# A ConvNeXt-V2 block on one core: the DRAM copy of the normalised image laid out by row pair and channel

## The chip, the core and the metric

The kernel runs on one core of a Trainium2 chip. The core has a matrix engine (TensorE, "PE" in the profile, with its weight loads as "PEld"), a vector engine (VectorE, "DVE"), an activation engine (ScalarE, "ACT"), a general engine (GpSimd, "POOL") and a queue processor (SyncE, "SP") that here only issues DMAs. Sixteen DMA engines move data between DRAM and the on-chip memory (SBUF); PE's results land in PSUM. The metric is device time in microseconds (us): the median of three runs was 1463.72 us before the change (1463.25 to 1465.25).

## The reference, cut to what matters

The input `x` has 512 x 512 pixels of 96 channels in bf16.

```python
out = sum(xp[:, i:i+H, j:j+W, :] * dw[i, j] for i in range(3) for j in range(3))  # depthwise 3x3
h = _layernorm(out, axis=-1)                    # over the 96 channels of a pixel
h = jnp.einsum('bhwc,ce->bhwe', h, w1)          # 96 -> 384
h = _gelu(h)
gx = jnp.sqrt((h * h).sum(axis=(1, 2), keepdims=True) + 1e-6)   # per channel, over ALL pixels
nx = gx / (gx.mean(axis=-1, keepdims=True) + 1e-6)
h = grn_gamma * (h * nx) + grn_beta + h
h = jnp.einsum('bhwe,ec->bhwc', h, w2)          # 384 -> 96
return x + h
```

The sum in `gx` runs over the whole image, so nothing can be put out before every pixel has gone through the first matmul and the gelu. That splits the kernel into two passes.

## The kernel before

**Blocks and quads.** The image is cut into 64 blocks of 8 rows (index `d`). Each block is two quads of 4 rows (index `b` or `q`, 128 in all).

**The first pass** works on a block in steps. Four DMAs load its pixels (`load_x`, tile `xin`). DVE transposes them 32 by 32 (`turn_x`, tile `xT`). PE does the 3x3 convolution on 32 x 32 tiles (`conv_taps`), and the result is stored as `y_bf` in two halves `ee`, each [128, 3, 512]: partition p = 32 q + 2 c + k holds row k of the row pair q, and channel c of sixteen; the three planes are the groups G of 32 channels, and `ee` is the channel's parity. POOL squares it (`stage_sq`), PE sums over channels (`stage_stats`), DVE forms the variance, POOL takes the inverse root by Newton steps (`stage_rstd`, `stage_newton`), DVE transposes the result (`stage_turn`, tile `rt`). SP writes it to DRAM in four small DMAs (`stage_rows`) and reads it back spread over the partitions in four more (`stage_bcast`, tile `rbc`). Statistics, rows and broadcasts are done for batches of two blocks. POOL then multiplies (`stage_norm`, tile `yn`, one instruction per half).

**The copy.** `yn` has channels and rows mixed on the partitions, while the matmul with `w1` needs 96 channels on 96 partitions. So SP writes `yn` to DRAM (`stage_write`: one DMA for the half `ee` = 0, two for `ee` = 1, whose row pairs are rotated by two) and reads it back as `ynT`, [96, 4, 512] for each quad (`stage_read`, `read_yn`: two DMAs per quad, one for each row pair). In DRAM the copy lies as `[d][plane ee*3+G][pair][32 x 512]`: six planes, 128 KB apart. The ring `yn_ring` holds six quads.

**The MLP.** PE multiplies a quad by `w1` and ACT applies the gelu (`mlp_units`, six units per quad, tile `g`). DVE (`bn_stats`) or PE (`gram_next`) gather the sums of squares. Every third quad ("whole") is also stored to DRAM as it is, in three DMAs of 512 KB (`store_next`, tensor `g_dram`), one per slot.

**The second pass** goes through the 128 quads in an order written out beforehand (`ORDER`). Whole quads are loaded from `g_dram` (POOL's queue, 1.5 MB); five are still held; for the other 85, less three that are kept on chip, `ynT` is read again (SP's queue, `read_yn`) and matmul and gelu are done again (`recompute`). PE multiplies by the scaled `w2` (`stage_mm2`), DVE adds the input and the bias (`xb`), and SP stores the result (`stage_out`).

**What sets the order.** Every instruction of the first pass stays in program order on its engine. A planner (`put`, L802 to L838) fills slots; a slot holds one MLP quad. For block `d` with its norm in slot s, an odd one: the write is in s+1, the reload of the even quad in s+2, of the odd quad in s+3, their MLPs in s+4 and s+5. Rows of a batch are two slots after its last statistics, broadcasts three, the first norm four. Inside a slot the loop from L857 on fixes what SP issues, one after the other. From slot 13 on, an odd slot has: x loads, a store, the reload of the even quad, rows; an even slot: the reload of the odd quad, broadcasts, first write, a store, two more writes. Before slot 13 ("early") the reloads come first and the x loads after the writes.

The built program gives SP's DMAs eight completion counters in turn: a DMA is issued only when the eighth one before it has landed, whatever else it waits for.

Of the kernel before, what the change touches and what calls it, by code (L numbers as in the profile page):

```python
# [12 lines left out]
GR = 4  # L13
# [40 lines left out]
def kernel(  # L54
# [13 lines left out]
    bf16 = x.dtype  # L68
    assert bf16 == mybir.dt.bfloat16

    B, H, W, C = x.shape
# [11 lines left out]
    QW = GR * 128  # L83
    NQ = GR * W // QW
    dram = ctx.enter_context(tc.tile_pool(name="dram", bufs=1, space=bass.MemoryType.DRAM))
    yn_dram = dram.tile([ND, 2 * NI, 4, 32 * W], bf16, name="yn_dram")
    r_dram = dram.tile([len(BATCHES), R8 * BATCH * W], bf16, name="r_dram")

    TAIL0 = NBLK - NTAIL
# [25 lines left out]
    def quad_out(flat_ap):  # L115
        return flat_ap.rearrange("p (g r m) -> p g r m", r=GR, m=MB)

    PLANE = 4 * 32 * W

    def read_yn(eng, t, q):  # L120
        base = yn_dram[q // 2]
        for h in range(2):
            eng.dma_start(out=t[:C, 2 * h:2 * h + 2, :].rearrange("c r w -> c (r w)"),
                          in_=bass.AP(base.tensor, base.offset + (2 * (q % 2) + h) * 32 * W,
                                      [[2 * W, 16], [PLANE, 2 * NI], [1, 2 * W]]))

    consts = ctx.enter_context(tc.tile_pool(name="consts", bufs=1))
    prepool = ctx.enter_context(tc.tile_pool(name="pre", bufs=1))
# [49 lines left out]
    with ExitStack() as p1:  # L178
# [242 lines left out]
            pool.dma_start(out=bet_bf[:], in_=grn_beta.rearrange("(j p) -> p j", p=128))  # L421

        def setup_ynt():
            for t in yn_ring:
                pool.memset(t[C:128, :, :].rearrange("p r w -> p (r w)").bitcast(f32), 0.0)

        def setup_mlp():
# [219 lines left out]

        def stage_write(d, ee):
            yn = yns.pop((d, ee))
            base = yn_dram[d]  # L650
            step = 64 if ee else 128
            for p0 in range(0, 128, step):
                sp.dma_start(out=bass.AP(base.tensor, base.offset + ee * NI * PLANE + (p0 + 64 * ee) % 128 * W,
                                         [[W, step], [PLANE, NI], [1, W]]),
                             in_=yn[p0:p0 + step, :, :])

        def stage_read(b):
            t = yn_ring[b % NYT]
            read_yn(sp, t, b)
            ynts[b] = t  # L660

        bsts = {}
        ents = {}
# [140 lines left out]
        def put(s, what, v):  # L804
            at.setdefault((s, what), []).append(v)
# [5 lines left out]
        for k, (d0, n) in enumerate(BATCHES):  # L811
            for d in range(d0, d0 + n):
                quick = 2 * d + 1 not in mlp_slots
                put(2 * d + 1 if quick else 2 * d + 2, "sqa" if quick else "sqp", d)
                put(2 * d + 2, "staty", d)
                last_s = 2 * d + 2 if quick else 2 * d + 3
                put(last_s, "statq", d)
            ramp = 2 * (d0 + n) <= RAMP
            if ramp:
                put(last_s, "chain", k)  # L820
                put(last_s + 1, "spread", k)
            else:
# [29 lines left out]
        def next_x(s):  # L852
            if s % 2 and (s + 7) // 2 <= ND:
                load_x((s + 7) // 2)

        alone = 0
        for s in range(last_slot + 1):  # L857
            get = lambda kind: at.get((s, kind), [])
            early = s < FIRST_MLP + 6
            if not early:  # L860
                next_x(s)
            if early or s % 2 == 0:
                for b in get("read"):
                    stage_read(b)
            for k in get("bcast"):
                stage_bcast(k)
            for d in get("write"):
                stage_write(d, 0)
            store_next()
            for d in get("write"):  # L870
                stage_write(d, 1)
            if early:
                next_x(s)
            elif s % 2:
                for b in get("read"):
                    stage_read(b)
            for k in get("rows"):
                stage_rows(k)
            for k in get("newton"):
                stage_rstd(k, pool)  # L880
                stage_newton(k, pool)
# [47 lines left out]
            else:  # L929
# [160 lines left out]
```

## Time and profile before

| What | Value |
|---|---|
| Median of three runs | 1463.72 us |
| The profiled execution | 1462.48 us, of which its span 1460.6 us |
| Busy: PE, ACT, POOL, DVE | 1334.5, 1333.3, 1299.0, 1080.6 us |
| First pass with all stages at work | about 100 to 850 us |
| Second pass | about 950 to 1460 us |
| SP's hardware queue (q1) | 178044 packets, 318.50 MB, 69.6% of 16 engines |
| `ynT<-yn_dram` | 420 DMAs of 192 KB |
| `yn_dram<-yn` | 64 DMAs of 384 KB, 128 of 192 KB |
| `g_dram<-g` | 114 DMAs of 512 KB |

Times on the profile are microseconds from the start of the span. A row of a group names line, engine, operation, output and input tiles. "L36" is the helper that records every instruction of the first pass, so groups are told apart by their tiles. "SPq" is SP's queue: an instruction there is the issue of a DMA, not the transfer. A line of the list of waits reads: who waited, for whom, total us, number of times, longest us. The share of DMA is the mean busy share of the 16 engines.

### The profile page before, as it was taken

To read this page: it belongs to the slowest core of one execution; us is meant where nothing else is said; L and a number is where in the kernel's file an instruction comes from. 1 tells how busy PE (TensorE), PEld (TensorE's weight loads), DVE (VectorE), ACT (ScalarE), POOL (GpSimd) and SP (SyncE) were. 2 spreads that over 40 slices of the span, in tenths; PEclk is the share of its full clock that TensorE was granted. 3 is DMA by queue.
4 is the path that set the end of the run, shared out by engine and by line. 5 is a ranking of instruction groups with operands and counts; after the bars stand their busy time and mean duration, and the time that the engine had idled before them with its cause. 6 is when DMAs were issued, how large, how long until landed. Compare 5 with 4: busy or idle time off the path is not lost.

```text
span 1460.6 us, 55999 instructions
## 1 busy us (share of the span) xinstructions
PE 1334.5 (91%) x24212; PEld 871.7 (60%) x24212; DVE 1080.6 (74%) x2052; ACT 1333.3 (91%) x1235; POOL 1299.0 (89%) x899
## 2 busy tenths in 40 slices
PE   7879999999999999989999987889999989899998
PEld 3445555555555555555555554567777667666676
DVE  5768988988889898888889878745555545455455
ACT  4879999999999999999999999989999888888897
POOL 3499999999999999999999995489999999899997
PEclk8899999999999999999999999999999999999999
DMA  7779899998899998999899766499999999999997
GB/s 175 212 219 283 275 286 274 277 287 269 271 299 272 277 290 268 281 280 275 261 275 299 228 190 192 162 355 331 344 373 391 393 383 362 378 378 370 395 366 303
DMA packets 194103, 430.82 MB, mean 295 GB/s; under 512 B 39184, under 2 KB 88944, under 8 KB 188992
## 3 DMA queue, kind: packets, MB, share of 16 engines
q1 hardware_dynamic: 178044, 318.50, 69.6%
q0 software_dynamic: 15616, 108.29, 19.9%
q8 instruction: 190, 3.11, 0.9%
q10 hardware_dynamic: 196, 0.45, 0.1%
q14 instruction: 57, 0.47, 0.1%
HBM read 265.70 MB, written 161.45 MB: 292 GB/s over the span
## 4 chain that ended last, share of the span: by engine, by line
PE 42%; DMA 22%; ACT 18%; POOL 7%; DVE 4%; issue 3%; SPq 2%; ACTq 0%; DVEq 0%; POOLq 0%
PE PS L36 42%; ACT g L36 13%; DMA out_dram<-o_sb 11%; DMA ynT<-yn_dram 7%; ACT y_bf L36 4%; POOL xb L339 3%; DMA xin<-in_x_dram 3%; SPq L36 2%; POOL yn L36 2%; DVE bst L36 2%; DVE o_sb L36 1%; POOL ysq L36 1%; DMA rbc<-r_dram 1%; ACT xT L36 1%; ACT ysq L36 0%
## 5 line engine op out<-in xcount | busy, mean ns | idle before, releaser
L36 ACT ACTIVATE g<-PS 128x1024 bf16<-128x1024 f32 (+1 forms) x722 | 705.5, 1055 | 34.3 <-PE PS L36 20.2
L36 DVE BATCH_NORM_STATS2 bst<-g 128x6 f32<-128x512 bf16 x885 | 547.0, 677 | 46.8 <-ACT g L36 46.7
L36 PE MATMUL PS<-ynT,w1p 128*128 128x512 bf16 x1920 | 544.8, 381 | 39.0 <-ACT g L36 23.0
L36 ACT ACTIVATE gr<-PS 128x1536 bf16<-128x1536 f32 x348 | 485.8, 1450 | 47.6 <-PE PS L36 42.3
L36 DVE TENSOR_TENSOR o_sb<-PS,xb 128x384 bf16<-128x384 f32 x512 | 275.7, 557 | 244.8 <-PE PS L36 172.2
L36 POOL TENSOR_TENSOR yn<-y_bf,rbc 128x1536 bf16<-128x1536 bf16 x124 | 382.3, 3104 | 14.2 <-DMA rbc<-r_dram 13.2
L339 POOL TENSOR_TENSOR xb<-xr,B2c 128x1536 f32<-128x1536 bf16 x118 | 368.4, 3132 | 17.2 <-DVE o_sb L36 15.7
L36 POOL TENSOR_TENSOR ysq<-y_bf 128x1536 bf16<-128x1536 bf16 x120 | 327.1, 2747 | 38.1 <-DVE y_bf L36 38.1
L36 PEld LDWEIGHTS <-gr 128*128 128x128 bf16 x4152 | 206.6, 99 | 82.6 <-issue 31.5
L36 PE MATMUL PS<-xT,Wq 32*32 32x511 bf16 (+1 forms) x9216 | 235.9, 396 | 10.7 <-DVE xT L36 3.8
L36 PEld LDWEIGHTS <-w1p 128*128 128x128 bf16 x1920 | 148.4, 98 | 152.6 <-issue 89.2
L36 PE MATMUL PS<-W2s,gr 128*128 128x96 bf16 x4080 | 216.6, 207 | 23.6 <-DVE o_sb L36 23.3
L36 PE MATMUL PS<-w1p,ynT 128*128 128x384 bf16 (+2 forms) x1272 | 192.7, 273 | 27.6 <-ACT g L36 22.2
L36 PEld LDWEIGHTS <-Wq 32*32 32x32 bf16 x9216 | 100.2, 89 | 142.8 <-issue 64.8
L36 PEld LDWEIGHTS <-g 128*128 128x128 bf16 x2626 | 161.9, 98 | 34.2 <-issue 4.2
L36 PE MATMUL PS<-g 128*128 128x128 bf16 (+1 forms) x2386 | 173.2, 222 | 1.8 <-DVE warm L36 1.2
L36 PEld LDWEIGHTS <-ynT 128*128 128x128 bf16 x1272 | 102.0, 97 | 105.2 <-issue 82.6
L36 ACT ACTIVATE y_bf<-PS 128x1024 bf16<-128x1024 f32 (+1 forms) x141 | 137.4, 984 | 25.2 <-PE PS L36 25.2
L36 DVE STREAM_TRANSPOSE xT<-xin 128x576 f32<-128x576 f32 (+1 forms) x195 | 145.0, 771 | 6.2 <-DMA xin<-in_x_dram 4.9
L36 PEld LDWEIGHTS <-gl 128*128 128x128 bf16 x1824 | 89.4, 98 | 32.3 <-issue 9.4
L36 PE MATMUL PS<-W2s,gl 128*128 128x96 bf16 x1824 | 96.5, 206 | 7.7 <-DVE o_sb L36 7.5
L36 DVE CAST y_bf<-PS 128x512 bf16<-128x512 f32 x115 | 78.1, 679 | 5.8 <-PE PS L36 5.1
(108 smaller groups left out, 571.6 us busy)
## 6 DMA issues: line engine op xcount, KB each, us to landing
ynT<-yn_dram SPq DMA_DIRECT2D x420, 192.0 KB
g_dram<-g SPq DMA_DIRECT2D x114, 512.0 KB
gl<-g_dram POOLq DMA_DIRECT2D x38, 1536.0 KB, 11.3
xin<-in_x_dram SPq DMA_DIRECT2D x253, 216.0 KB
out_dram<-o_sb SPq DMA_DIRECT2D x127, 384.0 KB
xr<-in_x_dram POOLq DMA_DIRECT2D x123, 384.0 KB, 7.1
yn_dram<-yn SPq DMA_DIRECT2D x64, 384.0 KB
yn_dram<-yn SPq DMA_DIRECT2D x128, 192.0 KB
```

The lines of the kernel that those rows point to most:

```text
L36: r = f(*a, **k)
L339: pq.tensor_tensor(out=xb[:], in0=grp[q]["xr"][:], in1=bias[:, None, :].to_broadcast([128, PXP, C]), op=ALU.add)
```

## The change

- The copy in DRAM is now `[quad][row pair][channel][2 rows x 512]`, with the channels in the order in which `ynT` has them. A row pair is 192 KB in one piece.
- A block is written with six DMAs: two for `ee` = 0 (one for each row of the pairs, 64 partitions two apart), four for `ee` = 1 (32 partitions each).
- A block is reloaded with one DMA of 768 KB into a pair of ring places; the ring is allocated as three pairs. In the second pass a quad is one DMA of 384 KB.
- Both quads are reloaded in slot s+2. From slot 13 on an odd slot issues: rows, the reload, x loads, broadcasts, a store; an even slot: six writes, a store. Broadcasts move from the third slot after the statistics to the second, behind the rows of the same slot.
- A whole quad is stored in two DMAs of 768 KB, one per slot, at the end of what SP issues in the slot.

```diff
-    yn_dram = dram.tile([ND, 2 * NI, 4, 32 * W], bf16, name="yn_dram")
+    yn_dram = dram.tile([NBLK, 2, C, 2 * W], bf16, name="yn_dram")
...
-    def read_yn(eng, t, q):
-        base = yn_dram[q // 2]
-        for h in range(2):
-            eng.dma_start(out=t[:C, 2 * h:2 * h + 2, :].rearrange("c r w -> c (r w)"),
-                          in_=bass.AP(base.tensor, base.offset + (2 * (q % 2) + h) * 32 * W,
-                                      [[2 * W, 16], [PLANE, 2 * NI], [1, 2 * W]]))
+    def read_yn(eng, t, q, n=1):
+        base = yn_dram[q]
+        eng.dma_start(out=t[:C].rearrange("c r w -> c (r w)"),
+                      in_=bass.AP(base.tensor, base.offset, [[2 * W, C], [2 * W * C, 2 * n], [1, 2 * W]]))
...
-    yn_ring = [prepool.tile([128, GR, W], bf16, name=f"ynT{i}") for i in range(NYT)]
+    yn_pairs = [prepool.tile([128, R8, W], bf16, name=f"ynT{i}") for i in range(NYT // 2)]
+    yn_ring = [yn_pairs[i // 2][:, GR * (i % 2):GR * (i % 2) + GR, :] for i in range(NYT)]
...
         def stage_write(d, ee):
             yn = yns.pop((d, ee))
-            base = yn_dram[d]
-            step = 64 if ee else 128
-            for p0 in range(0, 128, step):
-                sp.dma_start(out=bass.AP(base.tensor, base.offset + ee * NI * PLANE + (p0 + 64 * ee) % 128 * W,
-                                         [[W, step], [PLANE, NI], [1, W]]),
-                             in_=yn[p0:p0 + step, :, :])
+            base = yn_dram[2 * d]
+            np_ = 64 if ee else 128
+            for k in range(2):
+                for p0 in range(0, 128, np_):
+                    pair = (p0 // 32 + 2 * ee) % 4
+                    sp.dma_start(out=bass.AP(base.tensor, base.offset + pair * C * 2 * W + ee * NI * 2 * W + k * W,
+                                             [[2 * NI * 2 * W, np_ // 2], [2 * W, NI], [1, W]]),
+                                 in_=yn[p0 + k:p0 + np_:2, :, :])
-        def stage_read(b):
-            t = yn_ring[b % NYT]
-            read_yn(sp, t, b)
-            ynts[b] = t
+        def stage_read(d):
+            read_yn(sp, yn_pairs[d % (NYT // 2)], 2 * d, 2)
+            for b in (2 * d, 2 * d + 1):
+                ynts[b] = yn_ring[b % NYT]
...
-                put(last_s + 3, "bcast", k)
+                put(last_s + 2, "bcast", k)
...
+                put(s + 2, "read", d)
                 for b in (2 * d, 2 * d + 1):
-                    put(s + 2 if ramp else s + 2 + b % 2, "read", b)
...
-            if not early:
+            if early:
+                reads()
+            else:
+                rows()
+                reads()
                 next_x(s)
-            if early or s % 2 == 0:
-                for b in get("read"):
-                    stage_read(b)
+            for d in get("write"):
+                for ee in range(2):
+                    stage_write(d, ee)
+            if early:
+                store_next()
+                next_x(s)
+                rows()
             for k in get("bcast"):
                 stage_bcast(k)
-            for d in get("write"):
-                stage_write(d, 0)
-            store_next()
-            for d in get("write"):
-                stage_write(d, 1)
-            if early:
-                next_x(s)
-            elif s % 2:
-                for b in get("read"):
-                    stage_read(b)
-            for k in get("rows"):
-                stage_rows(k)
+            if not early:
+                store_next()
...
-                n = NCH * QW * NQ // 3
+                n = NCH * QW * NQ // 2
...
-                    stores.extend((b, h) for h in range(3))
+                    stores.extend((b, h) for h in range(2))
```

More of the change, by code (lines that the diff above doesn't have):

```diff
@@ L116, in quad_out @@
         return flat_ap.rearrange("p (g r m) -> p g r m", r=GR, m=MB)
-    PLANE = 4 * 32 * W
-    def read_yn(eng, t, q):
-        base = yn_dram[q // 2]
-        for h in range(2):
-            eng.dma_start(out=t[:C, 2 * h:2 * h + 2, :].rearrange("c r w -> c (r w)"),
-                          in_=bass.AP(base.tensor, base.offset + (2 * (q % 2) + h) * 32 * W,
-                                      [[2 * W, 16], [PLANE, 2 * NI], [1, 2 * W]]))
+    def read_yn(eng, t, q, n=1):
+        base = yn_dram[q]
+        eng.dma_start(out=t[:C].rearrange("c r w -> c (r w)"),
+                      in_=bass.AP(base.tensor, base.offset, [[2 * W, C], [2 * W * C, 2 * n], [1, 2 * W]]))
     consts = ctx.enter_context(tc.tile_pool(name="consts", bufs=1))
@@ L423, in setup_ynt @@
         def setup_ynt():
-            for t in yn_ring:
+            for t in yn_pairs:
                 pool.memset(t[C:128, :, :].rearrange("p r w -> p (r w)").bitcast(f32), 0.0)
@@ L859, with reads, rows @@
             early = s < FIRST_MLP + 6
-            if not early:
-                next_x(s)
-            if early or s % 2 == 0:
-                for b in get("read"):
-                    stage_read(b)
+            def reads():
+                for d in get("read"):
+                    stage_read(d)
+            def rows():
+                for k in get("rows"):
+                    stage_rows(k)
+            if early:
[3 more added lines that the diff above has]
+                reads()
+                next_x(s)
+            for d in get("write"):
[5 more added lines that the diff above has]
+                rows()
             for k in get("bcast"):
                 stage_bcast(k)
-            for d in get("write"):
-                stage_write(d, 0)
-            store_next()
-            for d in get("write"):
-                stage_write(d, 1)
-            if early:
-                next_x(s)
-            elif s % 2:
-                for b in get("read"):
-                    stage_read(b)
-            for k in get("rows"):
-                stage_rows(k)
+            if not early:
+                store_next()
             for k in get("newton"):
```

## The prediction

> **What bounds the kernel now.** I read the stages first, the first pass (200 to 800 us) and the second (1000 to 1440 us). Columns after the span: busy time of PE, weight loads, DVE, ACT and POOL, granted clock, DMA share, GB/s.
>
> ```profile
> 200.00:800.00 600.00, 560.70 (x11667) 341.18 (x11644) 537.69 (x989) 573.70 (x614) 570.90 (x417) 1.00 0.91 278
> 1000.00:1440.00 440.00, 414.63 (x6056) 307.45 (x6055) 232.58 (x433) 401.65 (x289) 411.71 (x249) 0.99 1.02 375
> ```
>
> The first pass has no slack engine: ACT 96%, POOL 95%, PE 93%, DMA 91%. In the second the DMA engines never rest (1.02), so only their work counts there. Next, who waits between 300 and 870 us:
>
> ```profile
> PE PS L36 <- DMA ynT<-yn_dram: 10.6, 13, 2.1
> POOL yn L36 <- DMA rbc<-r_dram: 9.2, 10, 1.6
> PEld L36 <- DMA ynT<-yn_dram: 3.7, 4, 0.9
> ```
>
> PE stands 14.3 us before a reload of yn. The whole run's list has the same two totals, so none of it lies before 300 us. What it costs shows in the norms on POOL, two per block of 8 rows, in two windows:
>
> ```profile
> L36 POOL TENSOR_TENSOR yn<-y_bf,rbc x25: 3079/3106/3124, 126.1 to 288.2; 128x1536 bf16<-128x1536 bf16 x25
> L36 POOL TENSOR_TENSOR yn<-y_bf,rbc x77: 3089/3105/3128, 303.7 to 828.6; 128x1536 bf16<-128x1536 bf16 x77
> ```
>
> The first row is 12 blocks in 162.1 us, 13.51 each; the second 38 blocks in 524.9 us, 13.81 each. The first pace is POOL's own work (a block's squares and norms, and half of a Newton chain). The loss against it is 0.30 x 38 = 11.5 us. Last, SP's timeline, POOL's norm and the PE wait about 405 us (start, duration; a row merges several issues and the gaps between):
>
> ```profile
> 398.69 3.54 SPq L36 DMA_DIRECT2D xin<-in_x_dram  x4
> 402.33 0.37 SPq L36 DMA_DIRECT2D g_dram<-g  x1
> 403.33 2.79 SPq L36 DMA_DIRECT2D ynT<-yn_dram  x4
> 406.22 1.48 SPq L36 DMA_DIRECT2D yn_dram<-yn  x1
> 407.80 0.43 SPq L36 DMA_DIRECT2D g_dram<-g  x1
> 408.32 1.95 SPq L36 DMA_DIRECT2D yn_dram<-yn  x2
> ```
> ```profile
> 398.21 6.18 POOL L36 TENSOR_TENSOR yn<-y_bf,rbc 128x1536 bf16<-128x1536 bf16 x2
> ```
> ```profile
> 409.69 1.02 PE L36 MATMUL PS<-ynT,w1p 128*128 128x512 bf16 x4 [0.41 <-DMA ynT<-yn_dram]
> ```
>
> POOL ends the block's norms at 404.39. SP, in order, is still issuing four reloads of the block before; the last write is out at 410.27, 5.9 us after the norm. The loop norm, write, reload, MLP has run out of slack because SP is late.
>
> **The change, part by part.** Issue costs on SP (min/median/max ns, 200 to 800 us):
>
> ```profile
> L36 SPq DMA_DIRECT2D ynT<-yn_dram x174: 541/589/1893, 210.8 to 800.0; - x174
> L36 SPq DMA_DIRECT2D yn_dram<-yn x132: 400/610/2307, 203.6 to 793.8; - x132
> L36 SPq DMA_DIRECT2D xin<-in_x_dram x176: 412/519/2134, 206.7 to 797.4; - x176
> L36 SPq DMA_DIRECT2D g_dram<-g x88: 339/428/1696, 204.3 to 798.0; - x88
> ```
>
> *SP's issues, per block.* Writes go from 3 to 6: +3 x 0.61 = +1.8 us (bounds 1.2 at the row's minimum, 6.9 at its maximum; the median, as the new ones are halves and quarters of those). Reloads go from 4 to 1: -3 x 0.59 = -1.8. The one reload has four times the pieces of an old one; an issue of it is bounded by 0.54 and 1.89, and I take 0.59, since the 384 KB write with as many pieces lies in a row whose median is 0.61. Stores go from 2 to 1.33: -0.3. Sum -0.3 us, nil on its own.
>
> *Order.* In the odd slot the reload is now first (behind the rows, every second block) and waits there for the writes to land. Behind it on SP stand four x loads, four broadcasts in every second block, and a store. The x loads are used four slots, 27 us, after their issue, and nobody waits for xin between 300 and 870 us: free. The broadcasts are issued right behind the x loads, a slot earlier than now, and are due two slots later; if that cover went, the 9.2 us above would stay. The rows are no longer behind x loads and reloads. The writes now have only broadcasts and a store before them, so I let them go out when their norm is ready: two at the end of the first half, four within 4 x 0.61 = 2.4 us of the second, against 5.9 above. That is 3.5 us of slack back per block. Today's lists show 28.9 us of SP waiting for writes to land, in 44 blocks; with the reload standing first I expect 100 to 150. That is waiting on an engine with nothing due.
>
> *What this wait does to the DMA engines.* Their work is 0.91 x 600 / 44 = 12.4 us per block. Between the landing of the writes and the first piece of the reload they have only what SP put behind the writes, a store half of 768 KB (2.8 us at 278 GB/s), in two slots of three. Uncovered, the hole is bounded by 0 and by 3.3 us, the one broadcast in the chain of waits that ran alone (issue to landing 3.27 us at 860 us, little data). I take 3 us in a third of the blocks, 1.0 on average: 12.4 + 1.0 = 13.4, just under POOL's 13.51. So POOL sets the pace again, and the loss of 11.5 us goes.
>
> *Ring in pairs.* The read of a block needs the pair of three blocks before; its MLP ended two slots earlier. The waits in the built program name the same matmul as before for each half in the second pass: no false dependency. Cost 0; bound 0 to 1.4 us once, at the ramp, where the first quad now waits for 384 KB more (at 278 GB/s).
>
> *Stores in halves.* Nobody waits for g_dram in the lists; 0.
>
> *Second pass.* One reload of 384 KB instead of two of 192. Here SP's eight completion counters, used in turn, make a DMA wait for the eighth before it: 22.6 + 9.2 + 9.1 + 8.9 = 49.8 us of waiting for out and ynT landings, which mostly goes. It gains nothing while the DMA engines are full; full they were. What could count is the pieces themselves, still 2 KB, now side by side instead of 128 KB apart. Queues in this stage:
>
> ```profile
> q0 software_dynamic: 13376, 94.31, 56.9%
> q1 hardware_dynamic: 31090, 69.84, 44.3%
> ```
>
> q0 moves 1.66 MB per percent. Of q1, 108 stores of 384 KB are 42.5 MB, at q0's rate 25.6%; the reloads' 26.7 MB took the other 18.7%, or 1.43 MB per percent. Bounds: at q0's rate they would take 16.1%, a gain of 2.6% of 440 us = 11.4 us (13 over the whole pass of 510 us); as much in the other direction. I take 0, as size, partitions and pieces per engine are those of before.
> [...] No run here shows a pitch's effect yet.
>
> *Sum.* -11.5 in the first pass from 300 to 829 us, -0.5 for the blocks behind it, 0 elsewhere: -12.0. The profiled execution is 1462.48 us (span 1460.6 and 1.9 around it), so 1450.5 there; the median of the runs is 1.2 above it, so **1452 us**.
>
> **The rivals.**
> *The hole decides (slower).* Place: SP, at the reload's wait in each odd slot. If a block's writes land late because the pieces are small, and no store covers, the engines idle 1.9 us per block rather than 1.0: 14.3 us per block, 0.5 above today's 13.81, x 54 blocks = +26, less the 3.5 us of slack won once: about 1486. It decides from a hole of 13.81 - 12.4 = 1.4 us. For it: DMA at 0.91, so little room. Against: two slots in three have a store behind the writes.
> [...] The trace agrees that these issues cost 0.6 us each, but it also has three reload issues that go; that size gets 0.02, inside the hole's 0.18.
> *The layout pays (faster).* Contiguous pieces bring the reload to q0's rate: 1452 - 13 = 1439. For it: the 14% lower rate. Against: 96 partitions, unchanged, may be the cause.
> *Nothing moves.* The slack is eaten by something else in the loop (newton, rows), or reloads get slower in the second pass by what the first wins: 1464. For it: ACT and POOL leave 4 to 5% in all. Against: 125 to 300 us ran at 13.51 with the same loop.
>
> **How the numbers follow.** My forecast 0.60, layout 0.10, hole 0.18, nothing 0.12 (0.07 within 0.2%, 0.05 above). 0.2% is 2.9 us, about what a measurement here tells from no change. The forecast's own range is 1446 to 1459, with 0.02 of its 0.60 within 0.2%. So faster 0.58 + 0.10 = 0.68, same 0.09, slower 0.23. The range leaves out the stronger half of the hole, a hole of over about 1.9 us (0.10), and the best of the layout (0.06): 1438 to 1484.
>
> **What would show it.** Right: norms 13.5 us per block through 829 us, PE's waits for ynT between 300 and 870 us from 14.3 to under 3, those of POOL for rbc near 0, writes issued within 3 us of the norm, SP's waits for yn_dram up to 100 or more, second pass at 375 GB/s within 1%. Wrong: GB/s under 278 and a falling DMA share between 200 and 800 us with blocks over 13.8 (the hole), or a second pass shorter or longer than 510 us by more than 4.

## The result and the profile after

The changed kernel took 1567.66 us (median of four runs, 1566.34 to 1575.45) against 1463.49 us for the kernel before on the same chip: a ratio of 1.0735, 95% interval 1.0681 to 1.0789. The prediction was 1452 us, with 1438 to 1484 as its range. It was wrong in sign and by 116 us.

The sum `gx`, which ends the first pass, stands at 1030.7 us instead of 934.4. From there to the end it is 536.4 us instead of 526.2. So 96 us were lost in the first pass and 10 in the second (profiled executions: 1568.82 us with a span of 1567.0, against 1462.48 and 1460.6).

The stages first, as in the prediction; the second row is moved by 96 us with the pass. Columns after the span: busy PE, weight loads, DVE, ACT, POOL, granted clock, DMA share, GB/s. The changed kernel:

```profile
200.00:800.00 600.00, 524.91 (x10345) 306.29 (x10344) 482.13 (x880) 513.15 (x545) 508.85 (x376) 0.95 0.92 248
1100.00:1536.00 436.00, 402.43 (x5845) 297.63 (x5843) 224.86 (x418) 388.23 (x279) 399.86 (x242) 0.99 1.02 368
```

Every engine does less in the same time, and the DMA engines are as busy as before (0.92 against 0.91) while they move 248 GB/s instead of 278. That pair, a full share at a lower rate, will matter below. The granted clock is 0.95 where it was 1.00. Who waits, 300 to 870 us (total us, times, longest), and the norms on POOL:

```profile
PEld L36 <- DMA ynT<-yn_dram: 39.2, 19, 3.7
PE PS L36 <- DMA ynT<-yn_dram: 37.5, 19, 3.6
POOL yn L36 <- DMA rbc<-r_dram: 32.5, 10, 4.0
POOL yn L36 <- DMA yn_dram<-yn: 30.8, 7, 6.2
```
```profile
L36 POOL TENSOR_TENSOR yn<-y_bf,rbc x72: 3089/3105/3132, 304.3 to 848.0; 128x1536 bf16<-128x1536 bf16 x72
```

PE's 37.5 us and its weight loads' 39.2 are the same 19 moments, so PE stands about 39 us before a reload where the kernel before has 11. (The prediction's 14.3 added 10.6 and 3.7 in the same way.) POOL waits 63 us, half of it for a buffer of `yn` whose write has not landed. The norms: 72 are 36 blocks, and from the first norm of the first to the second norm of the last (3.1 us behind its first) there are 543.7 us, so 540.6 / 35 = 15.4 us per block, where 13.51 was forecast.

SP's waits between 200 and 800 us, first two lines of the kernel before, then the changed kernel and its timeline near the place that the prediction shows:

```profile
SPq L36 <- DMA yn_dram<-yn: 28.9, 34, 1.9
...
SPq L36 <- DMA xin<-in_x_dram: 4.5, 14, 0.7
```
```profile
SPq L36 <- DMA ynT<-yn_dram: 73.6, 39, 3.7
SPq L36 <- DMA xin<-in_x_dram: 59.4, 125, 1.8
SPq L36 <- DMA yn_dram<-yn: 41.6, 54, 3.4
```
```profile
408.83 5.66 SPq L36 DMA_DIRECT2D yn_dram<-yn  x6
...
416.21 0.32 SPq L36 DMA_DIRECT2D ynT<-yn_dram  x1
...
419.46 7.48 SPq L36 DMA_DIRECT2D yn_dram<-yn  x6
```

POOL's norms there, and PE's wait (in brackets the idle time before the row and what ended it):

```profile
396.89 6.17 POOL L36 TENSOR_TENSOR yn<-y_bf,rbc 128x1536 bf16<-128x1536 bf16 x2
412.97 6.18 POOL L36 TENSOR_TENSOR yn<-y_bf,rbc 128x1536 bf16<-128x1536 bf16 x2 [4.50 <-DMA yn_dram<-yn]
```
```profile
407.88 1.89 PE L36 MATMUL PS<-ynT,w1p 128*128 128x512 bf16 x4 [3.26 <-DMA ynT<-yn_dram]
```

The norm that ended at 403.06 is written from 408.83 to 414.49: its last write leaves SP 11.4 us later, where it was 5.9 before and 2.4 was forecast. That is a bad block: the median over the blocks from 200 to 800 us is 8.4 us, against 5.7 before. And SP waits 133 us in all for reloads and x loads, of whose data it has no need: all 164 of these waits end on the completion counter that the DMA to be issued uses itself. SP's DMAs use eight such counters in turn: of the 1241 behind the first eight, 1237 have that of the eighth before (1357 of 1361 in the kernel before). In 1239 of the 1241 every landing record of the DMA before on the same counter lies ahead of the end of the issue, and in the other two all but one, which the trace does not have. The chain of waits shows how the two meet (start, duration, what):

```profile
402.26 9.30 DMA xin<-in_x_dram
...
412.85 3.27 DMA yn_dram<-yn
...
416.21 6.29 DMA ynT<-yn_dram
...
422.54 3.01 PE PS L36 x61
```

An x load that takes 9.3 us lets a write go, the write lets the reload go, and PE waits for the reload. The x loads that nobody was to wait for stand in the chain.

### The profile page after: what moved, and what is told of

Its sections match the earlier page's. It is cut to its first block, busy times and chain, and to the rows that moved or that the text cites. A ratio compares the mean times of both kernels' runs of the same rounds, so it can differ in the third digit from the quotient of the medians.

```text
span 1567.0 us, 55627 instructions
## 1 busy us (share of the span) xinstructions
PE 1371.0 (87%) x24212; PEld 877.3 (56%) x24212; DVE 1085.1 (69%) x2052; ACT 1338.4 (85%) x1235; POOL 1298.9 (83%) x896
## 4 chain that ended last, share of the span: by engine, by line
PE 39%; DMA 36%; ACT 13%; DVE 4%; issue 3%; POOL 3%; SPq 2%; ACTq 0%; DVEq 0%; POOLq 0%
PE PS L36 39%; DMA out_dram<-o_sb 14%; DMA ynT<-yn_dram 9%; ACT g L36 8%; DMA xin<-in_x_dram 7%; DMA yn_dram<-yn 3%; ACT y_bf L36 2%; SPq L36 2%; DVE bst L36 1%; DMA g_dram<-g 1%; DVE o_sb L36 1%; POOL yn L36 1%; ACT xT L36 1%; POOL ysq L36 1%; DMA rbc<-r_dram 1%
## 5 line engine op out<-in xcount | busy, mean ns | idle before, releaser
L36 PE MATMUL PS<-ynT,w1p 128*128 128x512 bf16 x1920 | 558.8, 391 | 87.5 <-DMA ynT<-yn_dram 62.6
L336 POOL TENSOR_TENSOR xb<-xr,B2c 128x1536 f32<-128x1536 bf16 x118 | 368.4, 3131 | 24.4 <-DVE o_sb L36 22.1
L36 PE MATMUL PS<-xT,Wq 32*32 32x511 bf16 (+1 forms) x9216 | 253.7, 416 | 23.2 <-issue 12.8
L36 PEld LDWEIGHTS <-gl 128*128 128x128 bf16 x1824 | 90.1, 98 | 34.0 <-issue 11.4
## 6 DMA issues: line engine op xcount, KB each, us to landing
gl<-g_dram POOLq DMA_DIRECT2D x38, 1536.0 KB, 11.4
```

The source lines that it names most:

```text
L36: r = f(*a, **k)
L336: pq.tensor_tensor(out=xb[:], in0=grp[q]["xr"][:], in1=bias[:, None, :].to_broadcast([128, PXP, C]), op=ALU.add)
```

## The experiments

Both kernels and fourteen more, with the readings used below. "To gx" and "behind" are the two passes of the profiled execution. The period is the time between the norms of blocks 10 and 48 over 38, in us per block. Share and GB/s are of the DMA engines from 200 to 800 us; the share adds up the times of their packets (it is 1.02 in the second pass of both kernels), so packets in flight together can hide empty moments. The ratio is to the kernel before timed beside each run on the same chip, whose medians were 1459.8 to 1463.5 us; differences in us below are from 1463.5. e1 to e5 and e7 were timed twice, e9 three times, e10 four, e11 six, e6 and e8 eight, e12 ten, e13 and e14 twelve times. Runs e3, e6, e9, e13 and e14 put the rows and channels of the copy in each other's places, so their times are those of the work and not of a usable result.

| Kernel | us | ratio to before, 95% | to gx | behind | period | share, GB/s |
|---|---|---|---|---|---|---|
| before | 1463.5 | | 934.4 | 526.2 | 13.73 | 0.91, 278 |
| after | 1567.7 | 1.0735 (1.0681 to 1.0789) | 1030.7 | 536.4 | 15.43 | 0.92, 248 |
| e1 order only | 1534.2 | 1.0512 (1.0425 to 1.0598) | 1007.1 | 528.3 | 15.08 | 0.86, 254 |
| e2 layout only | 1519.2 | 1.0409 (1.0323 to 1.0494) | 972.8 | 541.7 | 14.47 | 0.91, 263 |
| e3 after, three writes | 1550.5 | 1.0623 (1.0527 to 1.0718) | 1015.9 | 536.6 | 15.17 | 0.93, 252 |
| e4 after, x first | 1497.9 | 1.0263 (1.0193 to 1.0332) | 960.4 | 535.6 | 14.13 | 0.97, 272 |
| e5 before, six writes | 1529.1 | 1.0444 (1.0361 to 1.0528) | 996.0 | 535.7 | 14.92 | 0.87, 256 |
| e6 before, new addresses | 1453.5 | 0.9928 (0.9905 to 0.9951) | 927.1 | 529.9 | 13.52 | 0.93, 282 |
| e7 e1, x first | 1480.8 | 1.0115 (1.0059 to 1.0170) | 950.2 | 526.7 | 14.04 | 0.92, 271 |
| e8 e7, one reload | 1468.9 | 1.0051 (1.0017 to 1.0085) | 933.9 | 533.5 | 13.58 | 0.99, 280 |
| e9 e4, three writes | 1476.6 | 1.0110 (1.0064 to 1.0155) | 937.8 | 537.0 | 13.70 | 0.99, 279 |
| e10 before, reload ahead | 1638.5 | 1.1251 (1.1199 to 1.1304) | 1118.2 | 534.7 | 17.28 | 0.75, 222 |
| e11 before, one reload | 1507.6 | 1.0332 (1.0303 to 1.0360) | 971.4 | 531.4 | 14.49 | 0.88, 263 |
| e12 e11, rows first | 1462.4 | 0.9987 (0.9954 to 1.0021) | 931.9 | 534.2 | 13.51 | 0.98, 283 |
| e13 e6 again | 1455.3 | 0.9946 (0.9917 to 0.9976) | 925.8 | 530.3 | 13.51 | 0.93, 283 |
| e14 e13, one reload per quad behind gx | 1463.5 | 1.0007 (0.9982 to 1.0031) | 928.4 | 535.1 | 13.54 | 0.92, 281 |

### Order or layout: e1, e2, e3

e1 gives the kernel before the new order, the ring in pairs and the stores in halves, and keeps the copy with its three writes and four reloads. e2 gives it the new copy with six writes and one 384 KB reload per quad, in the old order. e3 is the changed kernel with the three old writes.

```diff
 e1, on before
+            if early:
+                reads()
+            else:
+                rows()
+                reads()
                 next_x(s)
...
+        def stage_read(d):
+            for b in (2 * d, 2 * d + 1):
+                read_yn(sp, yn_ring[b % NYT], b)
+                ynts[b] = yn_ring[b % NYT]
```
```diff
 e3, on after
-            for k in range(2):
-                for p0 in range(0, 128, np_):
...
+            step = 64 if ee else 128
+            for p0 in range(0, 128, step):
+                sp.dma_start(out=bass.AP(base.tensor, base.offset + ee * NI * (4 * 32 * W) + (p0 + 64 * ee) % 128 * W,
+                                         [[W, step], [(4 * 32 * W), NI], [1, W]]),
+                             in_=yn[p0:p0 + step, :, :])
```

> The order of the change (rows, reload of both quads, x loads, broadcasts, store; then writes, store; stores in halves) with the old copy: planes in DRAM, three writes, four reloads of 192 KB. If the order makes the loss (the reload's wait for the writes leaves the DMA engines empty), it stays within 15 us of the changed kernel's 1567. If the loss comes from the new copy (six writes, one reload, its addresses), it is back at 1452 to 1470. If SP's eight completion counters make it, this has 14 DMAs per block where the change has 11 beside rows and broadcasts, and so lies in between or higher.

> The new copy (six writes, one reload of 384 KB per quad, both passes) in the old order, stores in thirds. Order theory: within 8 us of the 1463.5 of before. Copy theory: 1520 or more, with reload packets of 130 ns rather than 104. The second pass is that of the changed kernel in any case: it tells whether the 10 us lost there (526 to 536 us) belong to the addresses of the reload.

> The changed kernel, with its block written in the old three DMAs to the same 768 KB of the copy; rows and channels land in each other's places, so the output is not the reference's, but bytes, pieces and waits are. If six writes holding the counters are the cause, 60 us or more of the 104 come back (1500 or less). If the order or the reload is, under 20.

The order alone loses 71 us (1463.5 to 1534.2). Putting the one contiguous reload in place of the four, in both passes, makes it 1550.5 (e3, 16 more), and the six writes 1567.7 (17 more). These are steps between medians, with intervals of 0.5 to 1% of the time on either side, so only the first is sure by itself. It is the largest, and it was to be the gain. SP's waits in e1 between 200 and 800 us:

```profile
SPq L36 <- DMA yn_dram<-yn: 102.2, 46, 4.7
```

The wait for the writes is 102.2 us, in the forecast's 100 to 150. But the DMA share falls to 0.86: in 15.08 us per block the engines are busy 13.0 and idle 2.1 by that share. And what stands behind the wait is late: POOL waits 62.5 us for broadcasts there, PE 24.6 for reloads. 1534 lies below the range that e1's first theory gave (1552 and up) and far above its second, so the order makes most of the loss and not all. The third theory, the completion counters, forecast a time in between, but from a wrong count: beside rows, broadcasts and stores both kernels have 11 DMAs per block (3 + 4 + 4 and 6 + 1 + 4). And SP's longest wait of that kind in e1, for x loads, is 13.8 us in all, so the counters do not make e1's loss. The six writes' share in e3, 17 us, is below the 20 that its expectation set against them.

The layout alone loses too (e2, 56 us, about the 1520 of its copy theory, though the reload's packets take 116 ns and not 130), which called for the parts of it to be taken one by one.

### The wait by itself: e10

e10 makes one move on the kernel before: in the odd slot the reload of the even quad stands ahead of the x loads and the store.

```diff
+            for b in get("read"):
+                stage_read(b)
             if not early:
                 next_x(s)
-            if early or s % 2 == 0:
-                for b in get("read"):
-                    stage_read(b)
...
-            elif s % 2:
-                for b in get("read"):
-                    stage_read(b)
```

> The kernel before with one thing moved: in odd slots the even quad's reload stands ahead of the x loads and the store, so that nothing is issued while SP waits for the writes to land. If that hole is what the order costs, 35 us or more come on top of before, SP's waits for the writes rise from 28.9 us to 90 or more between 200 and 800 us, and the DMA engines' share falls. If it is SP's load or the broadcasts' place, within 10 us of before.

It is the worst kernel of all, 1638.5 us. SP's waits for the writes between 200 and 800 us, its timeline around one of them, then two stretches of 2 us of the windows with the columns as above:

```profile
SPq L36 <- DMA yn_dram<-yn: 160.3, 39, 6.2
```
```profile
403.00 1.74 SPq L36 DMA_DIRECT2D yn_dram<-yn  x2
409.25 1.22 SPq L36 DMA_DIRECT2D ynT<-yn_dram  x2
```
```profile
404.00:406.00 2.00, 2.00 (x52) 1.30 (x51) 2.00 (x5) 2.00 (x3) 1.97 (x1) 1.00 1.02 359
...
408.00:410.00 2.00, 0.48 (x20) 0.39 (x16) 0.85 (x2) 1.08 (x2) 2.00 (x1) 1.00 0.02 6
```

SP's last write leaves at 404.7. It issues nothing until 409.25, and the DMA engines go from a full share to 0.02. The reload then starts on empty engines, and what they could have moved meanwhile, the x loads, is issued behind it from 410.90 on. By the share a block has 13.0 us of busy engines, as in e1, and 4.3 idle. The packet records give the same order: from 200 to 800 us no packet at all is in flight for 56.9 us in e10, 22.5 in e1, 15.7 in the changed kernel and 4.0 before.

That this place of the reload costs 175 us is shown. What the time is lost on is not. DMA engines that stand empty are one reading. The other is SP itself: its DMA instructions and its waits for landings fill 560 of the 600 us in e10, 559 in e1, 567 in the changed kernel and 551 before, but only 430 to 435 in e8, e9 and e12 below, which run at 13.5 to 13.7 us per block. By this reading a wait is lost on a queue that was late already. e5 speaks for it, since there the share falls to 0.87 with hardly a wait for landings. But e6 runs at 13.52 with 539 us, so a full SP is not slow in itself. No run separates the two.

### The cover back: e4, e7

e4 is the changed kernel with the four x loads ahead of the rows and the reload; e7 is the same two lines on e1.

```diff
+                next_x(s)
                 rows()
                 reads()
-                next_x(s)
```

> The changed kernel with the x loads ahead of rows and reload in the odd slot, so that the DMA engines have 864 KB to move while SP waits for the writes to land. If the hole is the cause, 60 us or more come back. If slower packets or the counters are, it stays within 20 us of 1567.

> The order of the change with the old copy (1534), but x loads ahead of rows and reloads. If the hole behind the writes is all that the order costs, it comes back to 1455 to 1470. With the change's own copy the same edit gave back 70 of 104 us. If the earlier, denser order costs in itself, it stays above 1490.

One moved call gives 70 us back in the changed kernel (1567.7 to 1497.9) and 53 of the 71 in e1 (1534.2 to 1480.8). In e4 the DMA share is 0.97, against 0.92 with the same DMAs. Two lines of SP's waits from 200 to 800 us in e4:

```profile
SPq L36 <- DMA ynT<-yn_dram: 43.3, 23, 3.7
...
SPq L36 <- DMA yn_dram<-yn: 7.4, 16, 1.7
```

The x loads run while the writes land, and by the time SP comes to the reload little is left to wait for: 7.4 us instead of 41.6. In e4 the records show 1.3 us with no packet in flight, against 15.7. e7 lies between its two forecasts (1455 to 1470, above 1490), so some of what the order costs, about 17 us, is not undone by the x loads. The waits for counters are still 103 us (43.3 for reloads, 37.7 for stores, 22.1 for x loads). So these explain less of the loss than the place of the x loads does. How much of the 70 us went through the counters and how much through empty or slow engines, these two runs do not separate.

### Six writes: e5, e9

e5 has six writes into the old planes and everything else as before; e9 is e4 with three writes.

```diff
 e5, on before
-            for p0 in range(0, 128, step):
...
+            for k in range(2):
+                for p0 in range(0, 128, step):
+                    sp.dma_start(out=bass.AP(base.tensor, base.offset + ee * NI * PLANE + (p0 + 64 * ee) % 128 * W + k * W,
+                                             [[2 * W, step // 2], [PLANE, NI], [1, W]]),
+                                 in_=yn[p0 + k:p0 + step:2, :, :])
```

> The kernel before with one thing changed: each block is written with six DMAs, two partitions apart, into the old planes. The copy alone (six writes, merged reloads, new addresses) cost about 60 us, 38 of them in the first pass and 15 in the second. If the six writes are its cause in the first pass, 25 us or more come here (1485 and up), and the second pass stays at 526. If merging or addresses are, within 8 us of before.

> The change with x loads first (1498) and its block written in the old three DMAs into the new copy (channels and rows in each other's places, so not the reference's output). Theory: beside the hole, what the change costs is the issue of three more writes on SP. Then 20 to 30 us come back, to 1465 to 1478, and blocks run at 13.6 us. If the new copy's packets cost by themselves, it stays above 1485.

Alone, six writes cost 66 us: the period rises by 1.2 us per block, most of the 1.8 us that three more issues take. e5's SP waits 13 us for landings between 200 and 800 us; it is simply late. Its second pass takes 535.7 us, not the 526 expected, with the code of before. From its timeline:

```profile
403.64 3.81 SPq L36 DMA_DIRECT2D yn_dram<-yn  x4
```

The writes of the second half take 3.81 us, where the two of the kernel before took 1.95. In the order with x first they cost 21 us (e9 to e4), in the changed kernel 17 (e3).

### The addresses and the single reload: e6, e8, e11, e12

e6 reads each row pair from 192 contiguous KB, still two DMAs per quad, and writes as before. e11 reloads a block with one 768 KB DMA from the old planes in the even quad's place. e8 does that in e7's order. e12 is e11 with the rows of the statistics issued right behind the x loads, ahead of the store and the reload.

```diff
 e6, on before
-                          in_=bass.AP(base.tensor, base.offset + (2 * (q % 2) + h) * 32 * W,
-                                      [[2 * W, 16], [PLANE, 2 * NI], [1, 2 * W]]))
+                          in_=bass.AP(base.tensor, base.offset + (2 * (q % 2) + h) * C * 2 * W,
+                                      [[2 * W, C], [1, 2 * W]]))
```
```diff
 e11, on before
-            read_yn(sp, t, b)
...
+            if b % 2 == 0:
+                base = yn_dram[b // 2]
+                sp.dma_start(out=yn_pairs[b // 2 % (NYT // 2)][:C].rearrange("c r w -> c (r w)"),
+                             in_=bass.AP(base.tensor, base.offset, [[2 * W, 16], [PLANE, 2 * NI], [32 * W, 4], [1, 2 * W]]))
```
```diff
 e12, on e11
                 next_x(s)
+                for k in get("rows"):
+                    stage_rows(k)
...
-            for k in get("rows"):
-                stage_rows(k)
+            if early:
+                for k in get("rows"):
+                    stage_rows(k)
```

> The kernel before with one thing changed: each reload of 192 KB takes one row pair out of 192 KB in one piece (channels side by side) instead of out of six planes 128 KB apart. Writes as before, so channels and rows land in each other's places and the output is not the reference's; bytes and waits are. If the addresses make the reload's packets slow, the second pass grows by 8 us or more and the reload packets of the first rise from 105 ns to 115 or more. If merging two reloads into one DMA does, nothing moves (within 5 us).

> As the run with x loads first and the old copy, but the block is reloaded with one DMA of 768 KB from the old planes (first pass only; the second is as before). It differs from the other in the merging alone, and from the changed copy with x loads first (1498) in addresses and six writes. If a merged reload makes its packets slow, they stand at 130 ns here too and the time is within 15 us of 1498 less the 9 us of the second pass. If not, 105 ns and the time of the other run.

> The kernel before with the first pass's four reloads of a block as one DMA of 768 KB, in the place of the even quad's, old planes and three writes. If SP's issues set the pace of before (13.73 us per block against POOL's 13.5), three issues less bring it to POOL's pace: 8 to 12 us less than before, 1452 or so, with packets of 130 ns that cost nothing. If slower packets cost, or SP was not the pace, no change or slower.

> The kernel before with one 768 KB reload of the old planes, as in the run with one reload, and the rows of the statistics issued right behind the x loads, ahead of the store and the reload; the result is the reference's. If the loss of that run (+3.3%, 14.49 us per block) comes from the rows standing behind 768 KB of reload, so that the broadcasts wait for them with nothing else queued, the period falls back to 13.5 to 13.7 us and the time to 1450 to 1465 us, and SP's wait for the rows (70 + 21 us between 200 and 800 us) falls under 30. If the loss comes from the single large reload itself (its packets, or the odd quad's reload that no longer stands between first write and rows), the period stays above 14.2 and the time above 1495 us.

The addresses are no harm: e6 is 0.7% faster, a case that its expectation did not have, at 13.52 us per block, with PE's wait for reloads down to 0.3 us. The row of the reload's issues gives the likely reason (min/median/max ns):

```profile
L36 SPq DMA_DIRECT2D ynT<-yn_dram x176: 304/445/2392, 208.1 to 794.1; - x176
```

The median issue is 0.445 us against 0.589, so 0.6 us per block less of SP, while the packets themselves take as long as before (103.4 ns against 104.6 in the trace's packet records). The shortest issue falls too, from 541 to 304 ns. That PE's waits go by this way is likely, not shown apart.

The single reload was a surprise. Alone it costs 3.3% (e11), where 8 to 12 us less was forecast, and its timeline shows a hole of another kind:

```profile
400.66 0.63 SPq L36 DMA_DIRECT2D ynT<-yn_dram  x1
401.33 2.48 SPq L36 DMA_DIRECT2D r_dram<-rt  x4
407.48 2.75 SPq L36 DMA_DIRECT2D rbc<-r_dram  x4
```
```profile
406.00:408.00 2.00, 2.00 (x58) 1.04 (x47) 2.00 (x4) 1.83 (x3) 2.00 (x1) 1.00 0.14 20
```

The rows are issued behind 768 KB of reload and land behind it (their packets run from 404.7 to 407.4 us, the reload's end at 406.2); the broadcasts wait for the rows (70.4 us of SP in 21 waits, 200 to 800 us; the 21 in e12's expectation is this count, not a time), with the rest of SP's queue behind them. In the kernel before, the odd quad's reload lay in that gap. e12, whose DMAs are e11's with the rows ahead, is level with the kernel before, and of SP's wait for the rows this is left (200 to 800 us):

```profile
SPq L36 <- DMA r_dram<-rt: 0.3, 1, 0.3
```

So the loss of e11 was the rows' place, not the size of the reload; what rows ahead are worth with four reloads was not run. e8 agrees: with x loads and rows ahead of one reload it is 12 us faster than with four (e7). It met neither forecast, since its reload's packets take 137 ns, as slow as the one theory said, and the kernel is still faster: slower packets did not go with a longer time here.

### The second pass: e13, e14

The changed kernel and the runs that share its second pass (e2, e3, e4, e9) took 535.6 to 541.7 us for it, nine others 526.2 to 535.7, so scatter could not be excluded. e13 is e6 again; e14 reads each quad of the second pass with one DMA of 384 KB.

```diff
-                    read_yn(sq, ynt, q)
+                    read_yn1(sq, ynt, q)
...
+    def read_yn1(eng, t, q):
+        base = yn_dram[q // 2]
+        eng.dma_start(out=t[:C].rearrange("c r w -> c (r w)"),
+                      in_=bass.AP(base.tensor, base.offset + 2 * (q % 2) * C * 2 * W,
+                                  [[2 * W, C], [2 * W * C, 2], [1, 2 * W]]))
```

> The run with the new addresses alone once more, as the base of the next one: each reload of 192 KB comes from one contiguous row pair, the writes are those of the kernel before, so the rows and channels land in each other's places and the result is not the reference's. Expected again 0.990 to 0.995 of the kernel before, with a second pass (from the sum gx to the end) of 526 to 532 us.

> As the run beside it, but each quad of the second pass is read with one DMA of 384 KB in place of two of 192 KB; the first pass is unchanged. The changed kernel and the four runs that share its second pass took 535.6 to 541.7 us for that pass in their profiles, nine kernels with two reloads per quad 526.2 to 535.7. Theory that the single reload costs: the second pass gets 5 to 10 us longer than beside it and the time 0.3 to 0.7% above it. Theory that these are only scatter between runs, or come from the state in which the first pass leaves the queues: within 0.2% of the run beside it, second pass 526 to 533 us. The prediction's 0 for this pass says the latter.

The medians of twelve runs each are 1455.27 and 1463.49 us: the single reload costs 8.2 us, and the two intervals in the table do not overlap. The two profiles are 7.4 us apart: 4.8 behind `gx` (530.3 to 535.1) and 2.6 before it, where the code is the same. A single profile can't carry this: e5, e10 and e12 have two reloads per quad and take 534.2 to 535.7. By which wait the larger DMA costs is not settled: SP's waits for landings behind `gx` go, as forecast, from 81.7 us in e13 to 1.1 in e14, and it gains nothing, since the DMA share from 1000 to 1440 us is 1.02 in both.

## Why the prediction was wrong

The step that failed is the order. The prediction named SP as the engine that is late, and then took 100 to 150 us of waiting on SP for free, but for a hole of 1.0 us per block in the DMA engines' work that was to stay under POOL's pace. The wait came, 102 us in e1, and the order cost 71 us.

**The first pass is paced by SP being late, and is worth 11.5 us: the pace right, the sum only in part.** e6, which only makes reloads cheaper to issue, and e12, which has fewer of them and the rows ahead, both run at 13.5 us per block; `gx` comes 7.3 and 2.5 us earlier, not 11.5. None of the sixteen went below the floor that the prediction read from POOL's own work, 13.51.

**Reload first, "waiting on an engine with nothing due": wrong, and the largest error, 71 of 104 us with the whole order; 53 of the 71 come back with the x loads alone (e7).** The size of the wait was right (102 us in e1), its price was not. SP's queue is nearly all that the DMA engines have in the first pass (90.3% of the 16 engines from 200 to 800 us before, 73.9% in e10). While it waits for writes that it has just issued, nothing follows them, as e10 shows without anything else changed (a share of 0.02 and 4.3 us idle per block). The prediction looked for the engine that needs SP's next instruction, and found none due. It priced the wait on the DMA engines alone, and too low, and not on SP's own time, which it had found short. Which of the two sets the price stays open.

**"The x loads ... nobody waits for xin: free": wrong.** The engine that uses the pixels, DVE, waits for them 4.6 us in all, before 100 us, and not at all from 100 to 1030 us. SP waits 59.4 us by its counters (200 to 800 us), and 73.6 for reloads. The kernel before had 4.5 and 1.2. The prediction used the eight counters for the second pass alone. Moved ahead, the same x loads are worth 70 us (e4), in which the counters' part is not known.

**The writes "within 2.4 us" of the norm: wrong.** They were 11.4 us behind it at the place shown, and 8.4 in the median block. Taking x loads and reloads from in front of them did not help, since now they wait until these have landed.

**The hole, 12.4 + 1.0 = 13.4: wrong, and not by the hole alone.** The sum leaves out what the engines idle already, 1.2 us per block before. Share times period gives, of busy and idle engine time per block: before 12.5 and 1.2; e1 13.0 and 2.1; e10 13.0 and 4.3; after 14.2 and 1.2. So by the share the idle part of the changed kernel is no larger than before, and the busy part grew by 1.7. A hole there is all the same, since 15.7 us of 600 have no packet in flight, against 4.0; at other moments more packets are in flight together, and the share hides it. The 12.4 is not a fixed amount of work that a hole can be added to. e11 and e12 have the same DMAs, at 12.8 and 13.2 us, and the busier one is 3% faster; e8 and e9 are at 13.4 and 13.6 with periods of 13.6 and 13.7. In the trace's packet records a packet of an x load takes 216 ns before, 265 in after, and 216 again in e4. How much of the longer packets in after is a cause, and how much only many transfers started together once SP is let go, is not settled.

**SP's issues, "nil on its own": wrong, by 66 us alone, 21 with x loads first (e9 to e4) and about 17 here, a step that is not sure by itself.** The size of a write was right, 0.602 us, and the one reload took even 0.33 instead of 0.59, below the bound of 0.54.

```profile
L36 SPq DMA_DIRECT2D yn_dram<-yn x234: 571/602/1637, 202.6 to 795.7; - x117
L36 SPq DMA_DIRECT2D ynT<-yn_dram x39: 312/326/689, 199.7 to 786.5; - x39
```

The saving and the cost fall in different places, by a reading of the order that no run tests apart. The three further writes stand between the norm and the reload, in the loop that sets the pace; what the reload saves comes where SP waits in any case. Splitting three writes into six costs 66 us by itself (e5), and its likely cause is SP's issues, since SP hardly waits for landings there (13 us from 200 to 800 us). The case that the prediction gave 0.02, three more issues of 0.6 us in each of 54 blocks with nothing saved, comes to 97 us and 1561 by estimate. That this lies near the result is chance: the six writes are about 17 of the 104.

**Ring in pairs, stores in halves, at 0: not tested apart.** They are in e1, e7 and e8, and e8 is 0.5% above the kernel before with all of them.

**The second pass, 0 within 11.4: off by 8 us, inside its bounds.** e14 shows it for the single reload. The changed kernel's 368 GB/s missed the 375 within 1%, and its other 2 us are within what the profiles scatter. The contiguous pieces, the other half of that term, were rightly worth nothing there: 2 KB packets of the reload in that pass take 99.4 ns before, where they lie 128 KB apart, and 99.5 in e13, where they lie side by side.

**The rivals.** "The hole decides" had the right sign and place, SP's wait in the odd slot, and a hole of 1.9 us per block, near the 2.1 of e1; its 1486 was too low by 82 us, because it kept the busy part at 12.4, where e1 has 13.0 and the changed kernel 14.2. Its sign, a falling share, did not show in the changed kernel (0.92). "The layout pays" had the right sign in the first pass for another reason (issue time, e6), not for the rate.

## What to carry to other kernels

Do not take an in-order queue that feeds the DMA engines for an engine with nothing due, least of all one that was found late: before a DMA that waits for a landing is moved ahead, list what is queued behind it, keep enough transfers issued in front to cover the landing (four x loads in front gave back 70 us in e4 and 53 in e7), and count also the waits for completion counters (133 us of SP's time for reloads and x loads, 200 to 800 us). Price a DMA that is split or merged in the place where it is issued, not over the whole block: here three reload issues of 0.59 us that went did not pay for three write issues of 0.60 that came, and the likely reason, which no run tests apart, is that SP waits where the reload stands. And the busy share of the DMA engines is no fixed amount of work: per block it went from 12.5 to 14.2 us here for nearly the same bytes, so a sum of work and hole can come out too low.

## What the runs showed that was not expected

**Short stalls of PE came with a clock of 0.50.** The granted clock in the changed kernel around the PE wait shown above (columns as before, the clock third from the end):

```profile
406.00:408.00 2.00, 0.12 (x1) 0.12 (x2) 0.00 (x0) 0.00 (x0) 2.00 (x1) 0.81 1.04 219
408.00:410.00 2.00, 2.00 (x16) 0.47 (x27) 0.00 (x0) 1.00 (x2) 0.47 (x1) 0.50 1.03 223
410.00:412.00 2.00, 2.00 (x74) 0.78 (x50) 1.95 (x4) 1.37 (x3) 0.00 (x0) 0.83 0.96 258
```

PE waits from 404.6 to 407.9 and in the clock's records the half clock lasts from 407.2 to 410.6, 3.4 us. From 100 to 930 us the changed kernel has 20 gaps between matmuls above 1.5 us, 54.7 us in all, and 88.7 us at half clock; the kernel before has three gaps with 6.0 us, and 3.4 us at half clock. The gaps that came on top are 48.7 us, and half of the added 85.3 us, an estimate by the clock of 0.50, is 42.7, together 91 of the 96 us lost up to `gx`. Taken from 100 us to `gx`, the same sum gives 66 us for 73 lost in e1, 73 for 62 in e5 and 207 for 184 in e10, so it is near and no more. e4, 34 us above the kernel before, has 24 us at half clock, and e12, level with it, none. That the clock adds to the loss is read from the records, not shown by a run that changes it alone. The trace of the changed kernel has 19 slow stretches from 100 to 930 us: 13 of 3.4 us, five of 6.8 and one of 10.2. Those at 315, 523 and 578 us stand behind gaps of 1.6 to 2.6 us. In a time as long as the shortest, 3.4 us, ahead of each of the 19, PE was busy for 23 to 55% by its instruction records. What starts a slow stretch is not shown.

**Full engines at a low rate.** In the first two of these rows the DMA share is 1.04 and 1.03 while 219 and 223 GB/s move; in e10 a share of 1.02 moved 359 (404 to 406 us).

**The issue of a DMA went with its addresses.** The median is 0.589 us for a reload of 192 KB from six planes and 0.445 from one contiguous piece (e6). For 768 KB it is 0.631 from the planes (e11) and 0.326 from contiguous KB.

None of the runs with a usable result beats the kernel before by more than can be measured; e12 is level with it.
